# Linear attention with a routed MoE behind it: the division by the denominator for three of four query items moved from VectorE to ScalarE

## The chip, the cores and the metric

The kernel runs on one core of a Trainium2 chip. The metric is device time in microseconds (us) of one execution. The core's engines work in parallel, each through its own stream of instructions in the order of the program: TensorE (PE in the profile, PEld for its weight loads), VectorE (DVE), ScalarE (ACT), GpSimd (POOL) and SyncE (SP, which issues most DMAs). They wait for one another through semaphores.

## The reference

```python
# 8 batches, 8 heads, 576 rows, head dimension 64, 128 features
def phi(x):
    proj = einsum('bhsd,df->bhsf', x, w_phi)
    proj = proj - max(abs(proj), axis=-1, keepdims=True)
    return concatenate([exp(proj), exp(-proj)], axis=-1)
q_p, k_p = phi(q), phi(k)
kv  = einsum('bhsf,bhsd->bhfd', k_p, v)
z   = sum(k_p, axis=2)
num = einsum('bhsf,bhfd->bhsd', q_p, kv)
den = einsum('bhsf,bhf->bhs', q_p, z)[..., None] + 1e-06
attn = num / den
# x = attn as 4608 rows of 512; top-1 MoE of 8 experts, 512 -> 1024 -> 512:
do_compute = x @ w_skip > 0;  e = argmax(x @ w_gate);  g = softmax(x @ w_gate)[e]
out = x + (g * relu(x @ w1[e]) @ w2[e]  where do_compute, else 0)
```

The change concerns `num / den`.

## The kernel before, in words

The first 340 us or so are the attention, the rest is the MoE over sorted rows. A *unit* is four heads of one batch; there are 16 units of keys and 16 of queries. Each is cut into five *items*: item 0 holds the last 64 of the 576 rows of the heads, items 1 to 4 the other 512 (two head pairs, two halves of the rows). A loop over steps `t` works on one key item and, six steps later, on the query item of the same number: transposed by VectorE (tile `xT`), projected by TensorE (`ps_P`, L321), row maximum and subtraction by VectorE (`m` L328, `u` L331), exponentials by ScalarE (`ek` L346 and L347 for keys; `eqt` and `eq` L373 and L374 for queries, these after a transposition by TensorE into the PSUM tile `ps_U`, L367), products with `v` or `kva` by TensorE. `kva` is kv with 10 more columns: 9 for router and skip scores, and z. So five steps make a cycle of some 20 us, in which one unit of keys and one of queries go through.

A query item is used in `st_use_q` (L487; item 0 in L466, which runs for odd batches alone): TensorE fills one PSUM bank `ps_O` with four blocks of 74 columns (64 of num, 9 scores, 1 den). Then `norm` runs on it: VectorE adds 1e-6 to the four denominators (`den`, L438), takes the reciprocal (`rec`, L442), multiplies the 4 x 64 columns into `xm` (L449; `xt` for item 0) and the 4 x 9 score columns into `lgm` (L450). There are two banks `ps_O` in this stage. They turn between the items, the column sums of the keys (`z`, L407, copied out as `zs` by ScalarE, L410), the making of `kva` (L420, L424), and the ranking of rows for the MoE (L584). `ps_U` has one bank.

The order of TensorE's work in steps 8 to 78 is that of the program (`manual_schedule`); in it, L407 of a unit stands directly ahead of L487 of item 4. Everything else in the attention stage, so DVE, ACT, POOL and SP throughout and PE after step 78, is put in order by the framework's scheduler, which also adds the semaphore waits: an instruction that reads a PSUM bank is kept apart from an instruction of another engine on the same bank.

Behind the second unit of each batch, `post` computes the router's decisions (VectorE, nine small instructions and two for the gate), and, four steps later, `rank` (L584 on TensorE, then small VectorE instructions). Odd batches hold five row tiles there, even ones four. The MoE's weights come by SP in chunks of 512 KB; each is split into a rounded part by ScalarE (L198) and a rest by VectorE or GpSimd (L203). The first rows of the MoE are transposed in L782 and copied by ScalarE (L785) and VectorE (L786) before the first expert matmul (L908).

Of the kernel before, what the change touches and what calls it, by code (L numbers as in the profile page):

```python
# [12 lines left out]
AF = mybir.ActivationFunctionType  # L13
ALU = mybir.AluOpType
# [4 lines left out]
P = 128  # L19
# [5 lines left out]
def kernel(  # L25
# [12 lines left out]
    nc = tc.nc  # L38
    B, H, S, D = q.shape
# [40 lines left out]
    def bank(tag):  # L80
        if not ps:
            return psa.tile([P, 512], F32, tag=tag, name="ps_" + tag, bufs=CFG["na"][tag])
        return ps[0].tile([P, 512], F32, tag=tag, name="ps_" + tag, bufs=NB[tag])
# [146 lines left out]
    with actx:  # L230
# [200 lines left out]
                )  # L431
            kva_of[u.g] = kva

        def norm(o, xdst, ldst, shape):

            den = small.tile([P, 4], F32, tag="den", name="den")
            rec = small.tile([P, 4], F32, tag="rec", name="rec")
            nc.vector.tensor_scalar(  # L438
                out=den.rearrange("p (t o) -> p t o", o=1), in0=o[:, :, NA1:NAUG],
                scalar1=1e-6, scalar2=None, op0=ALU.add,  # L440
            )
            nc.vector.reciprocal(out=rec, in_=den)  # L442
            rv = rec.rearrange("p (t o) -> p t o", o=1)
            a, c = shape

            def sh(x):
                return x.rearrange("p (a c) d -> p a c d", a=a)

            nc.vector.tensor_tensor(out=xdst, in0=sh(o[:, :, 0:D]), in1=sh(rv.broadcast_to([P, 4, D])), op=ALU.mult)  # L449
            nc.vector.tensor_tensor(  # L450
                out=ldst, in0=sh(o[:, :, D:NA1]), in1=sh(rv.broadcast_to([P, 4, NA1 - D])), op=ALU.mult)

        def st_use_q(u, i):
            if i == 0 and u.b % 2 == 0:
                return
            kva = kva_of[u.g]
            o = bank("O")[:, 0:4 * NAUG]
            ov = o.rearrange("p (t c) -> p t c", c=NAUG)
            if i == 0:

                for h in range(4):
                    pr, hd = h // 2, h % 2
                    for half in range(2):
                        for par in range(2):
                            g = u.g - NQ * (1 - par)
                            nc.tensor.matmul(  # L466
                                ov[par * 64:par * 64 + 64, h, :],
                                et_of[g][:, half, hd * P + pr * 64:hd * P + pr * 64 + 64], kva_of[g][:, half, h, :],
                                start=(half == 0), stop=(half == 1),
                            )  # L470
                if u.hq == 0:
                    xt_of[u.b // 2] = (
                        [xp.tile([P, 1, 4 * D + 2 * h], F32, tag="xt%d" % h, name="xt") for h in range(2)],
                        xp.tile([P, 1, H, E + 1], F32, tag="lgt", name="lgt"),
                    )
                xt, lgt = xt_of[u.b // 2]
                norm(ov, xt[u.hq][:, 0, 0:4 * D].rearrange("p (h a d) -> p a h d", h=2, d=D),
                     lgt[:, 0, u.hq * 4:(u.hq + 1) * 4, :].rearrange("p (a h) e -> p a h e", a=2), (2, 2))
                return
            pr, th = (i - 1) // 2, (i - 1) % 2  # L480
            e = u.e[i].rearrange("p a (j h c) -> p a j h c", j=2, h=2)
            h0 = u.hq * 4 + 2 * pr
            for j in range(2):
                for hd in range(2):
                    for half in range(2):
                        for s in range(2):
                            nc.tensor.matmul(  # L487
                                ov[s * 64:s * 64 + 64, 2 * j + hd, :],
                                e[:, half, j, hd, s * 64:s * 64 + 64], kva[:, half, 2 * pr + hd, :],
                                start=(half == 0), stop=(half == 1),  # L490
                            )
            if u.hq == 0 and i == 1:
                xm_of[u.b] = (
                    [xp.tile([P, 4, 4 * D + 2 * h], F32, tag="xm%d" % h, name="xm") for h in range(2)],
                    xp.tile([P, 4, H, E + 1], F32, tag="lgm", name="lgm"),
                )
            xm, lgm = xm_of[u.b]
            norm(ov, xm[u.hq][:, 2 * th:2 * th + 2, 0:4 * D].rearrange(
                "p a (h r d) -> p a r h d", h=2, d=D)[:, :, pr],
                 lgm[:, 2 * th:2 * th + 2, h0:h0 + 2, :], (2, 2))  # L500
            if i == 4:
                c = slice(0, 4 * D)
                if u.hq == 0:
                    def store_half(b=u.b, xm=xm):
                        nc.sync.dma_start(out=rowm[b][:, :, c], in_=xm[0])
                        if b % 2 == 1:
                            nc.sync.dma_start(out=rowt[b // 2][:, c], in_=xt_of[b // 2][0][0][:, 0])
                    later.append((now[0] + 2, store_half))
                else:
                    post(u.b)  # L510
# [194 lines left out]
        for dh in range(2):  # L705
            nc.scalar.dma_start(
                out=wsrc[dh * 64:dh * 64 + 64],
                in_=w_phi)
# [9 lines left out]
        def f_use(u, i):  # L718
            (st_use_k if u.kind == "k" else st_use_q)(u, i)
# [382 lines left out]
    for grp in CFG["seq"]:  # L1102
# [7 lines left out]
        for which, w, n in how:  # L1110
            for _ in range(n):
                x = slots[which]
                c = done.get((x, w), 0)
# [82 lines left out]
    with tc.manual_schedule():  # L1196
# [4 lines left out]
        for k, (w, x, c) in enumerate(steps):  # L1201
            kind, i = x
# [95 lines left out]
```

## Time and profile before

| | |
|---|---|
| median of 3 runs | 623.17 us (622.9 to 623.51) |
| the profiled execution | 620.68 us, of which 619.0 us are its span |
| mean granted TensorE clock | 0.982 |
| busy in the span | PE 570.2 us, DVE 512.0, POOL 360.5, ACT 330.4 |

The profile shows one execution. Its views are the page (busy time of each engine, and the span in 40 slices), groups of instructions, the list of waits, windows (busy time per engine in a stretch), and a timeline. In timelines a row is: start, duration, engine, line and operation, tile written and tiles read, shapes, number of instructions merged, and in brackets the idle time of the engine before it with the instruction that ended it. TensorE's instructions overlap, so a row's end can lie behind the start of the next row.

### The profile page before, as it was taken

Reading aid. Unit: us, or ns where it says so; the run is one execution under the profiler, and the core shown is the slowest. Engines: PE = TensorE matmul, PEld = TensorE weight load, DVE = VectorE, ACT = ScalarE, POOL = GpSimd, SP = SyncE. Lnnn points to the kernel's source line nnn. Section 1 sums busy time; section 2 is a strip of 40 time slices with the busy share of each in tenths; the row PEclk is TensorE's granted clock in tenths of the full one; section 3 lists DMA queues with packets and bytes.
Section 4 is the critical chain, followed back from the end, with each engine's and each line's share of the span. In section 5 each row is a group of like instructions: output and inputs, shape, how many; then the busy total and the mean of one; then the engine's idle time right before and its main releaser. Section 6 shows DMA issues by size and latency. Waiting matters only on the chain. (4 is left out here: it accounts for less than half of the span.)

```text
span 619.0 us, 18767 instructions
## 1 busy us (share of the span) xinstructions
PE 570.2 (92%) x7486; PEld 468.9 (76%) x7486; DVE 512.0 (83%) x1084; ACT 330.4 (53%) x649; POOL 360.5 (58%) x390
## 2 busy tenths in 40 slices
PE   4699999999999999999999898699999898999993
PEld 2477777777777677776777788598888787989892
DVE  5899999999989999999986699957688887956851
ACT  3466556456656556556446445324658554665630
POOL 5665565564744747456661657974468855559121
PEclk9999999999999999999999898979999899999998
DMA  9988888887667766423152789676767678597200
GB/s 157 161 140 162 185 184 177 192 188 139 144 151 158 162 131 143 123 70 102 37 191 94 209 302 309 221 249 182 223 225 248 233 248 290 182 314 237 88 19 29
DMA packets 250233, 108.33 MB, mean 175 GB/s; under 512 B 192417, under 2 KB 235553, under 8 KB 250144
## 3 DMA queue, kind: packets, MB, share of 16 engines
q1 hardware_dynamic: 245632, 97.58, 60.9%
q0 software_dynamic: 3200, 9.45, 4.4%
q8 instruction: 60, 0.98, 0.6%
q10 hardware_dynamic: 1312, 0.08, 0.1%
q14 instruction: 29, 0.24, 0.1%
HBM read 83.86 MB, written 24.02 MB: 174 GB/s over the span
## 5 line engine op out<-in xcount | busy, mean ns | idle before, releaser
L203 POOL TENSOR_TENSOR w<-wraw_c,w 128x256 fp32r<-128x256 f32 x124 | 114.6, 958 | 51.1 <-ACT w L198 51.1
L354 POOL TENSOR_TENSOR z<-ek 128x512 f32<-128x512 f32 x64 | 81.5, 1273 | 98.4 <-ACT ek L347 73.6
L198 ACT ACTIVATE w<-wraw_c 128x1024 fp32r<-128x1024 f32 x96 | 97.5, 1051 | 4.3 <-DMA wraw_c<-in_moe_w_dram 2.9
L203 DVE TENSOR_TENSOR w<-wraw_c,w 128x1024 fp32r<-128x1024 f32 x65 | 86.9, 1345 | 12.9 <-ACT w L198 10.7
L328 DVE TENSOR_REDUCE m<-ps_P 128x8 f32<-128x1024 f32 (+2 forms) x86 | 88.6, 1030 | 6.4 <-PE ps_P L321 6.2
L331 DVE TENSOR_TENSOR u<-ps_P,m 128x1024 f32<-128x1024 f32 (+2 forms) x86 | 88.8, 1033 | 3.1 <-DVE xTt L296 0.2
L321 PE MATMUL ps_P<-wsrc,xT 64*64 64x128 f32 x2048 | 77.9, 281 | 12.1 <-DVE xT L298 6.9
L487 PEld LDWEIGHTS ps_O<-kva,eq 128*64 128x64 f32 x2048 | 74.5, 136 | 16.5 <-issue 5.7
L487 PE MATMUL ps_O<-kva,eq 128*64 128x74 f32 x2048 | 77.6, 228 | 4.1 <-DVE lgm L450 4.0
L321 PEld LDWEIGHTS ps_P<-wsrc,xT 64*64 64x64 f32 x2048 | 56.7, 134 | 27.4 <-issue 18.4
L373 ACT ACTIVATE eq<-ps_U 128x512 f32<-128x512 f32 x64 | 37.9, 592 | 64.7 <-PE ps_U L367 64.2
L389 PE MATMUL ps_K<-ek,v 128*64 128x256 f32 x512 | 70.8, 394 | 0.0
L855 POOL DMA_INDIRECT out_dram<-o,si x22 | 28.8, 1310 | 63.9 <-DVE si L854 56.8
L922 PE MATMUL ps_O<-w,hh 128*128 128x512 f32 x160 | 64.2, 401 | 0.0
L346 ACT ACTIVATE ek<-u 128x512 f32<-128x512 f32 x64 | 40.4, 631 | 38.4 <-DVE u L331 23.0
L367 PE MATMUL ps_U<-ident,u 128*128 128x128 f32 x288 | 49.1, 287 | 2.5 <-DVE u L331 1.9
L298 DVE STREAM_TRANSPOSE xT<-raw 128x512 f32<-128x512 f32 x64 | 44.8, 702 | 5.8 <-PE ps_P L321 2.8
L926 PE MATMUL ps_O<-w,hh 128*128 128x512 f32 x120 | 47.3, 394 | 1.3 <-POOL w L203 1.3
L389 PEld LDWEIGHTS ps_K<-ek,v 128*64 128x64 f32 x512 | 31.9, 137 | 20.9 <-issue 11.3
L927 PE MATMUL ps_O<-w,hlo 128*128 128x512 f32 x120 | 47.2, 393 | 0.0
L909 PE MATMUL ps_P<-x,w 128*128 128x256 f32 x144 | 38.9, 299 | 4.7 <-DVE x L786 4.7
L358 POOL TENSOR_TENSOR z<-z 128x512 f32<-128x512 f32 x32 | 40.8, 1275 | 2.5
(259 smaller groups left out, 1206.6 us busy)
## 6 DMA issues: line engine op xcount, KB each, us to landing
wraw_c<-in_moe_w_dram SPq DMA_DIRECT2D x96, 512.0 KB, 4.0
raw<-in_k_dram SPq DMA_DIRECT2D x64, 144.0 KB, 3.3
raw<-in_q_dram SPq DMA_DIRECT2D x64, 144.0 KB, 4.4
v<-in_v_dram SPq DMA_DIRECT2D x64, 128.0 KB, 2.8
out_dram<-xm SPq DMA_DIRECT2D x16, 512.0 KB, 4.2
xrows<-xm SPq DMA_DIRECT2D x8, 516.0 KB, 4.3
xrows<-xm SPq DMA_DIRECT2D x8, 512.0 KB, 4.7
vt<-in_v_dram SPq DMA_DIRECT2D x32, 32.0 KB, 2.8
```

The lines of the kernel that those rows point to most:

```text
L198: nc.scalar.activation(out=hi, in_=raw, func=AF.Copy)
L203: eng.tensor_tensor(out=lo[:, r], in0=raw[:, r], in1=hi[:, r].bitcast(F32), op=ALU.subtract)
L321: nc.tensor.matmul(p[s * 64:s * 64 + 64, hd, (nj + j) * NF:(nj + j + 1) * NF], xT[r, g * P + s * 64:g * P + s * 64 + 64], wsrc[r], start=T ...
L328: nc.vector.tensor_reduce(out=m.rearrange("p (j h) -> p j h", h=2), in_=pv, axis=AX.X, op=ALU.max, apply_absolute_value=True)
L331: nc.vector.tensor_tensor(out=uu[:, 0:2 * nj, :].rearrange("p (j h) f -> p j h f", h=2), in0=pv, in1=m.rearrange("p (j h o) -> p j h o", h ...
L354: zeng.tensor_tensor(out=z, in0=e[:, 0:2, :], in1=e[:, 2:4, :], op=ALU.add)
L367: nc.tensor.transpose(t[:, tt * P:(tt + 1) * P], uu[:, tt, :], ident)
L389: nc.tensor.matmul(o[hd * 64:hd * 64 + 64, :], u.v[:, 2 * hd + pr, g * D:(g + 1) * D], u.e[i][:, 2 * j + hd, :], start=(g == 0), stop=False,)
L487: nc.tensor.matmul(ov[s * 64:s * 64 + 64, 2 * j + hd, :], e[:, half, j, hd, s * 64:s * 64 + 64], kva[:, half, 2 * pr + hd, :], start=(half ...
L922: nc.tensor.matmul(y[sub], hh[:, t], wh[:, fi, :], start=first, stop=False)
L926: nc.tensor.matmul(y[sub], hh[:, t], wl[:, fi, :], start=False, stop=False)
L927: nc.tensor.matmul(y[sub], hlo[:, t], wh[:, fi, :], start=False, stop=last)
```

## The change

For query items 1, 2 and 3 (not 0 and 4) the product L449 is replaced by four ScalarE instructions, one a head, each copying 64 columns from PSUM to `xm` with the reciprocal as scale. `den`, `rec` and `lgm` stay on VectorE. Line numbers behind it move by five (L450 becomes L455, L487 becomes L492, L563 becomes L568).

```diff
-        def norm(o, xdst, ldst, shape):
+        def norm(o, xdst, ldst, shape, act=False):
...
-            nc.vector.tensor_tensor(out=xdst, in0=sh(o[:, :, 0:D]), in1=sh(rv.broadcast_to([P, 4, D])), op=ALU.mult)
+            if act:
+                for j in range(4):
+                    nc.scalar.activation(out=xdst[:, j // c, j % c], in_=o[:, j, 0:D], func=AF.Copy, scale=rec[:, j:j + 1])
+            else:
+                nc.vector.tensor_tensor(
+                    out=xdst, in0=sh(o[:, :, 0:D]), in1=sh(rv.broadcast_to([P, 4, D])), op=ALU.mult)
             nc.vector.tensor_tensor(
                 out=ldst, in0=sh(o[:, :, D:NA1]), in1=sh(rv.broadcast_to([P, 4, NA1 - D])), op=ALU.mult)
...
-                 lgm[:, 2 * th:2 * th + 2, h0:h0 + 2, :], (2, 2))
+                 lgm[:, 2 * th:2 * th + 2, h0:h0 + 2, :], (2, 2), i in (1, 2, 3))
```

The scheduler then puts the instructions in another order. First VectorE, from the norm of item 2 to the norm of item 3 in one cycle. `[waits ...]` names the engines whose semaphores an instruction waits for; DVE_49 is VectorE's own, Activation_49 that of ScalarE. Before:

```order
L438 TENSOR_SCALAR den<-ps_O 128x4 [waits PE_49]
L442 RECIPROCAL rec<-den 128x4 [waits DVE_49]
L449 TENSOR_TENSOR xm<-ps_O,rec 128x2x2x64 [waits DVE_49]
L450 TENSOR_TENSOR lgm<-ps_O,rec 128x2x18
L298 STREAM_TRANSPOSE xT<-raw 128x512 [waits PE_49]
L328 TENSOR_REDUCE m<-ps_P 128x8 [waits PE_49]
L331 TENSOR_TENSOR u<-ps_P,m 128x1024 [waits DVE_49,Activation_49]
L438 TENSOR_SCALAR den<-ps_O 128x4 [waits PE_49]
L442 RECIPROCAL rec<-den 128x4 [waits DVE_49]
L449 TENSOR_TENSOR xm<-ps_O,rec 128x2x2x64 [waits DVE_49]
L450 TENSOR_TENSOR lgm<-ps_O,rec 128x2x18
L328 TENSOR_REDUCE m<-ps_P 128x8 [waits PE_49]
```

The same stretch of VectorE after:

```order
L438 TENSOR_SCALAR den<-ps_O 128x4 [waits PE_49]
L442 RECIPROCAL rec<-den 128x4 [waits DVE_49]
L298 STREAM_TRANSPOSE xT<-raw 128x512 [waits PE_49]
L455 TENSOR_TENSOR lgm<-ps_O,rec 128x2x18 [waits DVE_49,Activation_49]
L328 TENSOR_REDUCE m<-ps_P 128x8 [waits PE_49]
L331 TENSOR_TENSOR u<-ps_P,m 128x1024 [waits DVE_49]
L438 TENSOR_SCALAR den<-ps_O 128x4 [waits PE_49]
L442 RECIPROCAL rec<-den 128x4 [waits DVE_49]
L455 TENSOR_TENSOR lgm<-ps_O,rec 128x2x18 [waits DVE_49,Activation_49]
L328 TENSOR_REDUCE m<-ps_P 128x8 [waits PE_49]
```

The two products are gone, `lgm` of the changed items waits for ScalarE, and the transposition `xT` has moved ahead of `lgm` of item 2.

Second ScalarE, from the exponentials of a key item to the copy of `zs`, which is where item 3 falls. Before:

```order
L346 ACTIVATE ek<-u 128x4x128 [waits DVE_49]
L347 ACTIVATE ek<-u 128x4x128
L373 ACTIVATE eqt<-ps_U 128x256 [waits PE_49]
L374 ACTIVATE eqt<-ps_U 128x256
L410 ACTIVATE zs<-ps_O 128x256 [waits PE_49]
```

The same stretch of ScalarE after, which stands so in all cycles but the last:

```order
L346 ACTIVATE ek<-u 128x4x128 [waits DVE_49,Activation_49]
L347 ACTIVATE ek<-u 128x4x128
L373 ACTIVATE eqt<-ps_U 128x256 [waits PE_49]
L374 ACTIVATE eqt<-ps_U 128x256
L451 ACTIVATE xm<-ps_O,rec 128x64 [waits DVE_49]
L451 ACTIVATE xm<-ps_O,rec 128x64 x3
L410 ACTIVATE zs<-ps_O 128x256 [waits PE_49]
```

The four copies of item 3 stand behind `ek` and `eqt`; those of items 1 and 2 stand, in nearly all cycles, between or beside the two exponentials `eq` (L373 and L374) of a later query item.

Third ScalarE at the end of the attention, where the last query unit meets the first weights of the MoE. Before:

```order
L374 ACTIVATE eq<-ps_U 128x512
L198 ACTIVATE w<-wraw_c 128x1024 x4
L785 ACTIVATE x<-ps_U 128x4x128 x2
L547 ACTIVATE ex<-d 128x40
L785 ACTIVATE x<-ps_U 128x4x128 x2
```

The same place of ScalarE after:

```order
L374 ACTIVATE eq<-ps_U 128x512
L198 ACTIVATE w<-wraw_c 128x1024 x4
L451 ACTIVATE xm<-ps_O,rec 128x64 x8
L552 ACTIVATE ex<-d 128x40
L790 ACTIVATE x<-ps_U 128x4x128 x4
```

The copies of items 2 and 3 of the last unit stand behind four splits of weights, and all four `x` of the first expert rows behind `ex` of the last batch's router. On VectorE one split (L203) stands there ahead of the two `lgm`. On SP the store of the last batch's rows moves behind two loads of weights and four stores of `out`.

## The prediction

> **What bounds the kernel now.** I read the page first, then windows of 25 us, then the waits of the attention stage (25 to 340 us), then the timeline of one quiet cycle. The page's first row and two windows (columns: PE, PEld, DVE, ACT, POOL busy, granted clock, DMA share, GB/s):
>
> ```profile
> PE 570.2 (92%) x7486; PEld 468.9 (76%) x7486; DVE 512.0 (83%) x1084; ACT 330.4 (53%) x649; POOL 360.5 (58%) x390
> 50.00:75.00 25.00, 25.00 (x464) 19.33 (x464) 23.10 (x53) 14.38 (x35) 12.46 (x10) 1.00 0.87 167
> 275.00:300.00 25.00, 22.86 (x441) 17.57 (x439) 24.22 (x69) 14.15 (x33) 15.15 (x16) 1.00 0.21 70
> ```
>
> In the quiet window TensorE never pauses and VectorE is idle 1.9 us of 25. In the window with routing work VectorE is busiest (24.22) and TensorE idles 2.1 us. ScalarE has over 10 us free in both. So a shorter VectorE can give back only TensorE's idle time. The waits name it (waiting instruction, releaser, total us, times, longest):
>
> ```profile
> PE ps_O L487 <- DVE lgm L450: 4.0, 3, 1.4
> PE ps_O L584 <- DVE lgm L450: 2.2, 3, 0.7
> ACT ek L346 <- DVE u L331: 18.1, 15, 2.9
> ```
>
> TensorE waited 6.2 us for VectorE to release `ps_O`, in three cycles only (the ones after odd batches). That is about all the change can win. ScalarE, on its side, takes up `ek` as soon as VectorE has made `u`.
>
> **The change part by part.** What is removed, and the instruction that stays behind it:
>
> ```profile
> L449 DVE TENSOR_TENSOR xm<-ps_O,rec 128x256 f32<-128x256 f32 x64 | 27.1, 424 | 2.1 <-DVE rec L442 0.3
> L450 DVE TENSOR_TENSOR lgm<-ps_O,rec 128x36 f32<-128x36 f32 x64 | 11.8, 185 | 0.0
> ```
>
> 48 of 64 products go: 48 x 0.424 = 20.4 us of VectorE's busy time. Added are 192 ScalarE copies of 64 columns, four in a group. No row shows a copy with a column of reciprocals as scale. The nearest are the copies of `kva` from PSUM:
>
> ```profile
> 68.24 0.41 ACT L425 ACTIVATE kva<-ps_O 128x292 f32<-128x292 f32 x1
> 68.53 0.19 ACT L428 ACTIVATE kva<-ps_O 128x4 f32<-128x4 f32 x1
> 68.69 0.41 ACT L425 ACTIVATE kva<-ps_O 128x292 f32<-128x292 f32 x1
> ```
>
> 292 columns take 0.41 us and 4 take 0.19, so 64 take 0.24; the next starts 0.16 after the 4-column one, so 0.21 after one of 64. A group of four is then 3 x 0.21 + 0.24 = 0.87 us. If they overlap as the exponentials do (below: 0.60 long, next after 0.47, so 0.13 hidden) it is 0.6; with no overlap 4 x 0.24 = 0.96. I take 0.87, from the smallest copies. 48 groups are 42 us of ScalarE, which its idle time can hold. [...]
>
> What matters is not the load but the wait. In the new order `lgm` waits for ScalarE, and in VectorE's queue everything stands behind it: the next `m` and `u`, on which `ek` waits. [...] So the product is off VectorE's busy time but not off its path: where `lgm` came 0.34 us after `xm` began, it now comes after a group of 0.87 on an engine that may have other work. The quiet cycle before, TensorE first, then VectorE, then ScalarE:
>
> ```profile
> 58.82 1.10 PE L321 MATMUL ps_P<-wsrc,xT 64*64 64x128 f32 x32
> 61.20 1.20 PE L487 MATMUL ps_O<-kva,eq 128*64 128x74 f32 x32
> 63.73 0.64 PE L407 MATMUL ps_O<-z,ones_f 128*32 128x256 f32 x8
> 64.30 1.25 PE L487 MATMUL ps_O<-kva,eq 128*64 128x74 f32 x32
> ```
> ```profile
> 55.10 0.18 DVE L442 RECIPROCAL rec<-den 128x4 f32<-128x4 f32 x1
> ...
> 56.33 0.96 DVE L328 TENSOR_REDUCE m<-ps_P 128x6 f32<-128x768 f32 x1 [0.49 <-PE ps_P L321]
> ...
> 57.43 0.92 DVE L331 TENSOR_TENSOR u<-ps_P,m 128x768 f32<-128x768 f32 x1
> ...
> 58.55 0.18 DVE L442 RECIPROCAL rec<-den 128x4 f32<-128x4 f32 x1
> ...
> 59.55 0.71 DVE L298 STREAM_TRANSPOSE xT<-raw 128x512 f32<-128x512 f32 x1 [0.27 <-PE ps_P L321]
> 60.19 1.19 DVE L328 TENSOR_REDUCE m<-ps_P 128x8 f32<-128x1024 f32 x1
> 61.48 1.23 DVE L331 TENSOR_TENSOR u<-ps_P,m 128x1024 f32<-128x1024 f32 x1
> ...
> 62.81 0.18 DVE L442 RECIPROCAL rec<-den 128x4 f32<-128x4 f32 x1
> ...
> 63.36 0.18 DVE L450 TENSOR_TENSOR lgm<-ps_O,rec 128x36 f32<-128x36 f32 x1
> ```
> ```profile
> 55.58 0.58 ACT L373 ACTIVATE eq<-ps_U 128x512 f32<-128x512 f32 x1
> 56.05 0.59 ACT L374 ACTIVATE eq<-ps_U 128x512 f32<-128x512 f32 x1
> ...
> 58.99 0.60 ACT L373 ACTIVATE eq<-ps_U 128x512 f32<-128x512 f32 x1 [2.25 <-PE ps_U L367]
> ...
> 62.74 0.63 ACT L346 ACTIVATE ek<-u 128x512 f32<-128x512 f32 x1 [0.73 <-DVE u L331]
> ...
> 63.80 0.36 ACT L373 ACTIVATE eqt<-ps_U 128x256 f32<-128x256 f32 x1
> 64.06 0.37 ACT L374 ACTIVATE eqt<-ps_U 128x256 f32<-128x256 f32 x1
> ```
>
> The same cycle after, hop by hop (0.1 from ScalarE to VectorE and for the small steps between; 0.05 from `rec` to ScalarE):
> - Item 1: `rec` is there at 55.28, ScalarE free behind its first `eq` at 56.05. Group to 56.92, `lgm` at 57.0, `m` at 57.1 instead of 56.33. `u` follows 1.1 later (57.43 - 56.33): 58.2 to 59.1. `rec` of item 2 ends 0.38 behind `u`, as before (58.73 behind 58.35): 59.5.
> - Item 2: group 59.55 to 60.42, `lgm` 60.5, `m` 60.6 instead of 60.19. `xT` fits into this wait, so it costs nothing here. `u` 1.29 after `m`: 61.9 to 63.1.
> - Item 3: `ek` at 63.15, `eqt` ends 1.69 later as before (62.74 to 64.43), the group starts 0.1 ahead of that end: 64.74 to 65.61; `lgm` 65.7 to 65.88. TensorE's L487 of item 4 needs that bank (the one of item 3, since L407 has the other). Release 0.15 behind: 66.03 instead of 64.30.
>
> TensorE stalls 1.75 us in a quiet cycle, with nothing in its queue to fill it, and as it was never idle there the cycle grows by that. ScalarE's idle time covers the other uses: the `eq` exponentials that are delayed by a group had 2.25 us of idle time ahead of L373. With a group of 0.6 the stall is 1.2, with 0.96 it is 2.05.
>
> 13 cycles in TensorE's written order meet L487 of items 3 and 4:
> - 7 quiet ones: 7 x 1.75 = 12.3 us.
> - 3 with the ranking of an even batch: `xT` stands behind `lgm` of item 2 there, so its 0.64 (59.55 to 60.19) is no longer hidden, and some 0.35 of small ranking steps are added: 2.75 each, 8.3 us.
> - 3 with an odd batch, late before already: the wait at item 4 grows by 1.75, that at L584 by 0.63 (0.87 + 0.1 in place of the product's 0.34), both on top of the 0.7 and 1.4 seen: 2.4 each, 7.2 us.
>
> The last two cycles and the last query unit, where PE's order is the scheduler's: an estimate of 3 us, from two stalls of 1.5 (0 to 4). Then the end of the attention:
>
> ```profile
> 335.37 3.63 PE L487 MATMUL ps_O<-kva,eq 128*64 128x74 f32 x96
> 344.70 0.56 PE L909 MATMUL ps_P<-x,w 128*128 128x256 f32 x1
> 336.50 3.90 ACT L198 ACTIVATE w<-wraw_c 128x1024 fp32r<-128x1024 f32 x4
> 340.49 1.72 DVE L203 TENSOR_TENSOR w<-wraw_c,w 128x1024 fp32r<-128x1024 f32 x1 [0.52 <-POOL w L203]
> ```
>
> The three L487 of the first row follow each other at 1.2 us. Now the third needs item 2's bank, whose copies stand behind the four splits (340.4) and whose `lgm` behind the split on VectorE (342.2): it starts at 342.5, not 337.8, 4.7 late. The router's `ex`, the `x` copies and the experts, steady from 344.70, come after it. I take 4.5; 0 if the first weights are late anyway, 6 with the later `x`. The two loads of weights that SP now issues ahead of the last store only gain; behind these, the MoE is as before.
>
> Sum: 12.3 + 8.3 + 7.2 + 3 + 4.5 = 35.3 us. Against the profiled execution's own 620.68: 656.0; against the median of the runs, 2.5 higher, 623.17 + 35.3 = 658.5.
>
> **The rivals.**
> - *Faster: the group hides.* TensorE's 6.2 us of waits go, the time is 617. It speaks for this that ScalarE is half idle and VectorE saturated where those waits are. It decides at `lgm` of item 3: the group would have to end by 63.3, and `eqt` ahead of it in the queue ends at 64.43. Chance 0.05.
> - *Only item 3 costs.* If VectorE gains enough lead from TensorE's stalls to hide items 1 and 2, the chain is `eqt` 64.43 - 0.1 + 0.87 + 0.43 (`lgm` and its hops) = 65.6: 1.3 a cycle, 17 us, less the 6.2, plus 3 for the end: 637. Against it: `m` in quiet cycles already waits for TensorE, so a lead is of no use there. Chance 0.14.
> - *The clock drops as well.* After long waits TensorE ran slow:
>
> ```profile
> 393.30 0.50 PE L926 MATMUL ps_O<-w,hh 128*128 128x512 f32 x1 [1.28 <-POOL w L203]
> 395.00:400.00 5.00, 3.46 (x19) 2.69 (x17) 4.97 (x4) 2.98 (x4) 5.00 (x4) 1.00 0.87 292
> 403.17 0.58 PE L909 MATMUL ps_P<-x,w 128*128 128x256 f32 x1 [4.71 <-DVE x L786]
> 405.00:410.00 5.00, 5.00 (x61) 4.91 (x60) 1.41 (x3) 1.52 (x2) 4.51 (x8) 0.58 0.76 229
> ```
>
> A wait of 1.28 us left the clock at 1.00, one of 4.71 brought it to 0.58 for 5 us, a loss of 2.1. My six long stalls (2.7 to 3.2) lie between: 6 x 2.1 = 12.6, so 671. [...] Chance 0.10.
> - *No effect*, if ScalarE's groups and `lgm` land where `xm` and `lgm` did: 623. `rec` to `lgm` is 0.55 now (62.81 to 63.36), less than a group. Chance 0.03.
>
> **How the numbers follow.** The forecast, VectorE held behind ScalarE in every cycle, has 0.68, and 658.5 is its sum. Its own range: groups of 0.6, with nothing for the end, 13 x 0.55 = 7 less and 7.5 less, 644; groups of 0.96, 13 x 0.3 = 4 more and 2.5 more for the end, 665. To leave out no more than 2 in 10 the range reaches down to the second rival and up to just short of the third: 636 to 669. A measurement of this kernel tells about 0.2% (1.2 us) from no change. Slower: 0.68 + 0.14 + 0.10 = 0.92; same 0.03; faster 0.05.
>
> **What would show it.** Right: `lgm` L455 on VectorE idle before it, waiting for ScalarE's `xm`; TensorE's waits for `lgm` in L492 up from 4.0 us to over 20, in all cycles, about 1.75 each; VectorE's busy time down by 20 us and ScalarE's up by some 40; a copy of 0.24 us every 0.21; the first L913/L914 run 35 us later than 344.70; the MoE behind it as long as before. Wrong: `lgm` not idle, or the waits at L492 only in the routing cycles, or a stage clock below 1.00, or copies over 0.3 us apart.

## The result, and the profile after

The changed kernel takes 668.86 us (median of 4 runs, 665.28 to 673.09), against 623.34 for the kernel before beside it: a ratio of 1.075, 95% interval 1.070 to 1.080. The forecast was 658.5. The direction and the waits came out as forecast, but the time is 10 us above the sum. The range ended at 669: 668.86 lies just below that, and the ratio on the 623.17 that the range started from (670) just above it. Nearest is the third rival, in which TensorE's clock drops as well (671). The profiled execution took 670.12 us, 668.4 of them its span, 49.4 more than the span before.

The page's first row and its row of granted clocks, then the two windows that the prediction showed of before (columns as there):

```profile
PE 585.1 (88%) x7486; PEld 479.1 (72%) x7486; DVE 496.5 (74%) x1036; ACT 367.9 (55%) x841; POOL 356.7 (53%) x390
...
PEclk9899979979989999899899979997999999999998
50.00:75.00 25.00, 23.32 (x414) 17.72 (x405) 19.95 (x39) 16.20 (x46) 11.45 (x9) 1.00 0.90 176
275.00:300.00 25.00, 21.45 (x388) 17.04 (x388) 17.02 (x36) 15.92 (x47) 11.22 (x10) 0.93 0.43 102
```

VectorE lost 15.5 us of busy time (512.0 to 496.5) and ScalarE got 37.5 more, but in the quiet window TensorE, which never paused before, now idles 1.7 us. In the other window it idles 3.6, and the clock there is 0.93, where it was 1.00: one of the signs that the prediction had named as showing it wrong. TensorE is even *busier* in all (570.2 to 585.1) with the same 7486 matmuls: some of them ran slowly (the 32 of L492 at 91.15 in 2.24 us, those at 67.98 in 1.25).

The groups of the change, from the page, and the waits from 25 to 382 us:

```profile
L451 ACT ACTIVATE xm<-ps_O,rec 128x64 f32<-128x64 f32 x192 | 44.3, 322 | 18.5 <-DVE rec L442 14.2
...
L455 DVE TENSOR_TENSOR lgm<-ps_O,rec 128x36 f32<-128x36 f32 x64 | 12.2, 192 | 54.9 <-ACT xm L451 54.9
```
```profile
DVE lgm L455 <- ACT xm L451: 54.9, 37, 2.4
PE ps_O L492 <- DVE lgm L455: 30.2, 13, 3.1
...
PE ps_O L589 <- DVE lgm L455: 4.4, 3, 1.5
```

VectorE's small score product, which never waited before, stands 54.9 us idle for ScalarE. TensorE's wait for that product was 6.2 us (4.0 + 2.2) and is 34.6. The same quiet cycle as in the prediction, the second half of it, ScalarE, VectorE and TensorE:

```profile
65.10 0.63 ACT L346 ACTIVATE ek<-u 128x512 f32<-128x512 f32 x1 [0.70 <-DVE den L438]
65.63 0.62 ACT L347 ACTIVATE ek<-u 128x512 f32<-128x512 f32 x1
66.15 0.36 ACT L373 ACTIVATE eqt<-ps_U 128x256 f32<-128x256 f32 x1
66.42 0.37 ACT L374 ACTIVATE eqt<-ps_U 128x256 f32<-128x256 f32 x1
66.68 0.93 ACT L451 ACTIVATE xm<-ps_O,rec 128x64 f32<-128x64 f32 x4
```
```profile
65.11 0.18 DVE L442 RECIPROCAL rec<-den 128x4 f32<-128x4 f32 x1
67.64 0.20 DVE L455 TENSOR_TENSOR lgm<-ps_O,rec 128x36 f32<-128x36 f32 x1 [2.36 <-ACT xm L451]
```
```profile
65.72 0.64 PE L407 MATMUL ps_O<-z,ones_f 128*32 128x256 f32 x8
67.98 1.21 PE L492 MATMUL ps_O<-kva,eq 128*64 128x74 f32 x31 [1.63 <-DVE lgm L455]
```

`rec` of item 3 is there at 65.29. ScalarE begins the copies at 66.68, since `ek` and `eqt` stand ahead of them in its queue. VectorE waits through all of it, with the next `m` behind the wait in its queue, and TensorE finds the bank closed for 1.63 us.

### The profile page after: what moved, and what is told of

It reads as the page before. It is cut to its first block, busy times and chain, and to the rows that moved or that the text cites. A ratio compares the mean times of both kernels' runs of the same rounds, so it can differ in the third digit from the quotient of the medians.

```text
span 668.4 us, 18918 instructions
## 1 busy us (share of the span) xinstructions
PE 585.1 (88%) x7486; PEld 479.1 (72%) x7486; DVE 496.5 (74%) x1036; ACT 367.9 (55%) x841; POOL 356.7 (53%) x390
## 5 line engine op out<-in xcount | busy, mean ns | idle before, releaser
L203 POOL TENSOR_TENSOR w<-wraw_c,w 128x256 fp32r<-128x256 f32 x124 | 111.0, 930 | 52.1 <-ACT w L198 52.0
L492 PE MATMUL ps_O<-kva,eq 128*64 128x74 f32 x2048 | 82.6, 235 | 36.4 <-DVE lgm L455 34.9
L492 PEld LDWEIGHTS ps_O<-kva,eq 128*64 128x64 f32 x2048 | 78.7, 143 | 49.7 <-issue 41.7
L203 DVE TENSOR_TENSOR w<-wraw_c,w 128x1024 fp32r<-128x1024 f32 x65 | 86.2, 1335 | 14.6 <-ACT w L198 11.7
L321 PE MATMUL ps_P<-wsrc,xT 64*64 64x128 f32 x2048 | 83.2, 293 | 10.5 <-DVE xT L298 7.0
L321 PEld LDWEIGHTS ps_P<-wsrc,xT 64*64 64x64 f32 x2048 | 60.6, 142 | 27.0 <-issue 19.0
L373 ACT ACTIVATE eq<-ps_U 128x512 f32<-128x512 f32 x64 | 38.0, 594 | 66.1 <-PE ps_U L367 65.9
L389 PE MATMUL ps_K<-ek,v 128*64 128x256 f32 x512 | 72.6, 400 | 0.0
L451 ACT ACTIVATE xm<-ps_O,rec 128x64 f32<-128x64 f32 x192 | 44.3, 322 | 18.5 <-DVE rec L442 14.2
L367 PE MATMUL ps_U<-ident,u 128*128 128x128 f32 x288 | 51.7, 300 | 1.7 <-ACT eqt L374 1.3
L455 DVE TENSOR_TENSOR lgm<-ps_O,rec 128x36 f32<-128x36 f32 x64 | 12.2, 192 | 54.9 <-ACT xm L451 54.9
## 6 DMA issues: line engine op xcount, KB each, us to landing
wraw_c<-in_moe_w_dram SPq DMA_DIRECT2D x96, 512.0 KB, 4.7
out_dram<-xm SPq DMA_DIRECT2D x16, 512.0 KB, 4.7
xrows<-xm SPq DMA_DIRECT2D x8, 512.0 KB, 4.8
```

Source lines behind the costliest of these rows:

```text
L203: eng.tensor_tensor(out=lo[:, r], in0=raw[:, r], in1=hi[:, r].bitcast(F32), op=ALU.subtract)
L321: nc.tensor.matmul(p[s * 64:s * 64 + 64, hd, (nj + j) * NF:(nj + j + 1) * NF], xT[r, g * P + s * 64:g * P + s * 64 + 64], wsrc[r], start=T ...
L367: nc.tensor.transpose(t[:, tt * P:(tt + 1) * P], uu[:, tt, :], ident)
L389: nc.tensor.matmul(o[hd * 64:hd * 64 + 64, :], u.v[:, 2 * hd + pr, g * D:(g + 1) * D], u.e[i][:, 2 * j + hd, :], start=(g == 0), stop=False,)
L492: nc.tensor.matmul(ov[s * 64:s * 64 + 64, 2 * j + hd, :], e[:, half, j, hd, s * 64:s * 64 + 64], kva[:, half, 2 * pr + hd, :], start=(half ...
```

## The experiments

Each shows its edit against the changed kernel, what was expected, and what came out. The ratios are to the kernel before on the same chip, whose median was 622.79, 621.11 or 622.11 us; each heading or its first lines say which.

### Item 3 alone (beside 622.79)

```diff
-                 lgm[:, 2 * th:2 * th + 2, h0:h0 + 2, :], (2, 2), i in (1, 2, 3))
+                 lgm[:, 2 * th:2 * th + 2, h0:h0 + 2, :], (2, 2), i == 3)
```

> ScalarE's copies only for item 3 of every four; items 1 and 2 go back to VectorE. Theory A (VectorE's lgm product must wait until ScalarE has left the same bank, and ScalarE works in order: at item 3 its group stands behind the copies of ek and eqt, so VectorE, and TensorE behind it, are held): item 3 of a quiet cycle still costs about 1.4 us, a ranking cycle about 2 to 2.4, and the end of attention about 4; TensorE's waits for lgm at item 3 stay near 1.6 and 2 to 3 us; the time is 640 to 650. Rival B (each of the three items costs the same share of the 45.5 us): 638 at most, with waits for lgm at item 3 of about 0.6 us.

Measured: 649.15 us, ratio 1.044 (1.039 to 1.050). Its waits from 25 to 365 us:

```profile
PE ps_O L492 <- DVE lgm L455: 24.0, 13, 3.3
PE ps_O L589 <- DVE lgm L455: 2.2, 3, 0.7
```

A quiet cycle's wait is 1.26 us, those of the ranking cycles are 1.7 to 3.3. Item 3 alone makes more than half of the loss, inside theory A's range. The wait at L589 is as before: that one belongs to item 1.

### Items 1 and 2 alone (beside 622.79)

```diff
-                 lgm[:, 2 * th:2 * th + 2, h0:h0 + 2, :], (2, 2), i in (1, 2, 3))
+                 lgm[:, 2 * th:2 * th + 2, h0:h0 + 2, :], (2, 2), i in (1, 2))
```

> ScalarE's copies only for items 1 and 2 of every four; item 3 goes back to VectorE. Theory A: no wait of TensorE for lgm in the quiet cycles, about 0.7 to 1.5 us in the ranking cycles, the end of attention still 4 us later; granted clock back at about 1.00 there; the time is 627 to 634. Rival B (what counts is ScalarE's added load or the number of copies): two thirds of the 45.5 us stay, about 653.

Measured: 632.47 us, ratio 1.016 (1.010 to 1.022), as theory A had it. It keeps two thirds of the added copies and a fifth of the loss, so the loss does not go by the number of copies or by ScalarE's load. TensorE has no wait for `lgm` in a quiet cycle; those in ranking cycles are 1.0 to 1.8, and the steady stream of expert matmuls (the first L914 of an unbroken row, L909 before) begins 24.2 us behind the last L407, against 19.3 before.

### Item 1 alone (beside 621.11), item 2 alone (beside 622.11)

Two kernels, with one of the two added lines each:

```diff
-                 lgm[:, 2 * th:2 * th + 2, h0:h0 + 2, :], (2, 2), i in (1, 2, 3))
+                 lgm[:, 2 * th:2 * th + 2, h0:h0 + 2, :], (2, 2), i == 1)
+                 lgm[:, 2 * th:2 * th + 2, h0:h0 + 2, :], (2, 2), i == 2)
```

> ScalarE's copies for item 1 of every four only, in the changed order (copies ahead of lgm). Theory: nothing stands ahead of item 1's copies in ScalarE's queue in the quiet cycles, and 0 to 1 us in the ranking cycles; up to 3 us there and 0 to 4 at the end: 623 to 629. Rival (each item a third of the loss): 638.

> ScalarE's copies for item 2 of every four only, in the changed order (copies ahead of lgm). Theory: in ScalarE's queue two eq copies stand ahead of item 2's, no ek, so VectorE's wait is short and falls in slack; the cost is at the end of attention (items 1 and 2 cost 4.8 us there, item 1 alone 1.2): 624 to 628. Rival (additive thirds): 638.

Measured: item 1 630.07 us, ratio 1.015 (1.013 to 1.017), above what I expected; item 2 622.36, ratio 1.001 (0.9995 to 1.003), just under it. The miss on item 1 is in its queue. VectorE's timeline in a ranking cycle, then ScalarE's:

```profile
77.22 0.18 DVE L442 RECIPROCAL rec<-den 128x4 f32<-128x4 f32 x1
79.27 0.20 DVE L455 TENSOR_TENSOR lgm<-ps_O,rec 128x36 f32<-128x36 f32 x1 [1.88 <-ACT xm L451]
```
```profile
77.21 0.42 ACT L346 ACTIVATE ekt<-u 128x256 f32<-128x256 f32 x1 [1.96 <-DVE den L438]
77.53 0.40 ACT L347 ACTIVATE ekt<-u 128x256 f32<-128x256 f32 x1
77.84 0.58 ACT L373 ACTIVATE eq<-ps_U 128x512 f32<-128x512 f32 x1
78.32 0.92 ACT L451 ACTIVATE xm<-ps_O,rec 128x64 f32<-128x64 f32 x4
```

Two `ekt` and an `eq` stand ahead of item 1's copies, where I had expected nothing in quiet cycles and up to 1 us in ranking ones. VectorE waits 1.88 us here, and 1.73 in a quiet cycle. In quiet cycles it makes that up: TensorE waits for no `lgm` there. In ranking cycles it has nothing to make it up with (24.2 of 25 us busy before), and is still late 8 us on, where TensorE waits for the product of item 3, which VectorE makes alone here:

```profile
87.04 1.25 PE L492 MATMUL ps_O<-kva,eq 128*64 128x74 f32 x32 [1.12 <-DVE lgm L455]
```

So the three items alone cost 27.6, 9.3 and 0.7 us by their ratios (of 622.79, 621.11 and 622.11), 37.6 together, where the change as a whole costs 45.5. The 8 that are over appear only when the delays come together, and the traces say that most of it is TensorE's clock: between 25 us and the last L407 it falls six times in the changed kernel (twice for 6.83 us and four times for 3.41, some 10 us of cost, two sections below), twice with item 3 alone (3.41 us each, some 2.6 of cost) and never with item 1 or item 2 alone.

### The score product ahead of the copies (beside 622.79)

`scores` is the product that makes `lgm`, as a function of its own:

```diff
             if act:
+                scores()
                 for j in range(4):
...
-            nc.vector.tensor_tensor(
-                out=ldst, in0=sh(o[:, :, D:NA1]), in1=sh(rv.broadcast_to([P, 4, NA1 - D])), op=ALU.mult)
+            if not act:
+                scores()
```

> All three items as in the changed kernel, but VectorE's lgm product is written ahead of ScalarE's four copies, so that ScalarE waits for VectorE and not the other way round. Theory A1 (the whole loss is VectorE's wait in front of lgm): TensorE's waits for lgm are gone and the time is 623 or less. Theory A2 (also the bank that item 3 holds comes free late, since its copies still stand behind ek and eqt in ScalarE's queue, and the next transposes need the bank): TensorE waits about 1.1 us in each quiet cycle on xm in place of lgm; 640 to 645. Rival B (ScalarE's load itself): 665 to 670.

Measured: 638.65 us, ratio 1.027 (1.019 to 1.034): theory A2, a little under its range. All 192 copies are there. Those of item 3 have the same place in ScalarE's queue; the scheduler puts those of item 1 one `eq` later, and those of item 2 behind the `eq` and two `ek`. So at items 1 and 2 more than the wait changed, at item 3 the wait alone. 30 us of the loss are gone. What is left at TensorE is the bank, now held by the copies (25 to 365 us), and the quiet cycle of above, 0.94 us for 1.63:

```profile
PE ps_O L497 <- ACT xm L456: 20.0, 14, 4.7
```
```profile
66.86 1.25 PE L497 MATMUL ps_O<-kva,eq 128*64 128x74 f32 x32 [0.94 <-ACT xm L456]
```

The longest, 4.7, is in the last unit, behind the splits of the first expert weights. The other 15.3 stand against 34.6 in the changed kernel, 19.3 less. None is over 1.84 us, and the clock stays at 1.00 in all these cycles, which is worth the 10 us of the next section: together nearly all of the 30.

### The same z matmuls three times over, to fill the wait (beside 622.79)

```diff
-            for h in range(4):
+            for h in 3 * list(range(4)):
                 nc.tensor.matmul(zb[h * 32:(h + 1) * 32, 0:2 * NF], ones_f, u.z[2 + 2 * (h // 2)][:, h % 2, :],
```

> The changed kernel, with the four z matmuls of line 407 issued three times over (the same values written again), so that TensorE has about 1.1 us of work inside the stretch in which it else waits for lgm. If about 10 us of the loss are the clock that falls to 0.50 after waits of 3 us: the waits at line 492 shrink to about 0.5 and 1.9 us, the clock stays near 1.00 behind them, and the time falls to 657 to 662 in spite of the added work. If the clock has no part in it: 668 or above.

Measured: 661.89 us, ratio 1.064 (1.059 to 1.070). With 256 matmuls more the kernel is faster than the changed one. The waits got shorter (L492 30.2 to 17.9, and L589 4.4 to 2.6; 0.77 in a quiet cycle and 1.89 to 2.27 in a ranking one, a little more than expected), but the added work takes that back: from L407 to L407, the two kinds of cycle in which neither kernel has a low clock take 21.79 and 22.36 us in the changed kernel, and 22.77 and 21.78 here. What is gained lies in the cycles with a low clock. Three cycles hold the ranking of an even batch. The time from TensorE's L492 behind the wait to its next L407, the same work each time and with no wait between, was 19.42, 19.52 and 19.51 us before; in the changed kernel it is 21.98, 20.81 and 20.81; here it is 19.53, 20.83 and 19.53; and with item 3 alone 19.53 three times. The first of the changed kernel:

```profile
91.15 2.24 PE L492 MATMUL ps_O<-kva,eq 128*64 128x74 f32 x32 [3.02 <-DVE lgm L455]
...
113.13 0.64 PE L407 MATMUL ps_O<-z,ones_f 128*32 128x256 f32 x8
```

32 matmuls took 2.24 us where 1.25 is usual. Now TensorE's windows, cut at the points where the clock changes (columns: length, PE busy, matmuls, granted clock, DMA share, GB/s). The changed kernel first:

```profile
45.89:49.30 3.41, 1.90 (x40) 1.00 0.97 203
49.30:52.71 3.41, 3.38 (x50) 1.00 0.87 142
...
86.86:90.27 3.41, 1.27 (x36) 1.00 0.67 189
90.27:93.68 3.41, 2.53 (x34) 0.50 0.56 125
93.68:97.10 3.42, 3.42 (x39) 0.50 1.10 178
...
182.43:185.84 3.41, 0.33 (x13) 1.00 0.12 26
185.84:189.25 3.41, 3.41 (x48) 0.50 0.35 59
```

Item 3 alone, then the filled kernel:

```profile
129.57:132.98 3.41, 1.55 (x40) 1.00 0.54 122
132.98:136.40 3.42, 2.02 (x44) 1.00 0.02 5
...
218.31:221.72 3.41, 0.35 (x11) 1.00 0.08 18
221.72:225.14 3.42, 3.42 (x48) 0.50 0.37 61
```
```profile
181.46:184.87 3.41, 1.46 (x38) 1.00 0.02 6
184.87:188.28 3.41, 3.41 (x40) 0.51 0.72 114
```

In these traces the clock changes only on a grid of 3.41 us (every low spell that lies between 25 and 376 us in the twelve traces lasts 3.41 or 6.83), and a stretch is at 1.00 or at 0.50 (0.51 where my window is not exact). In these rows what follows a stretch goes by how much TensorE worked in it: 1.27, 0.33, 0.35 and 1.46 us of 3.41 are followed by 0.50, and 1.90, 1.55 and 2.02 are not. The wait of 3.26 us with item 3 alone was cut by the grid into two stretches with 1.86 and 1.40 of pause, and cost no clock; one of 3.34 us fell almost whole into one stretch (218.31), and did. A stretch with 43% of work (1.46 of 3.41) was still followed by 0.50. In the changed kernel all six waits of 3.0 to 3.1 us were followed by a low stretch: twice of 6.83 us, which cost 2.4 each (21.98 - 19.53 is the one shown), and four times of 3.41, which cost about 1.3 each (20.81 - 19.53).

### The last unit as before (beside 621.11)

```diff
-                 lgm[:, 2 * th:2 * th + 2, h0:h0 + 2, :], (2, 2), i in (1, 2, 3))
+                 lgm[:, 2 * th:2 * th + 2, h0:h0 + 2, :], (2, 2), i in (1, 2, 3) and u.g < NU - 1)
```

> The changed kernel, but the last of the 16 query units as before (no copies by ScalarE there). Theory: the wait of 4.7 us at the last matmuls of attention and the low clock behind it go, 4.5 to 7 us less than the changed kernel: 662 to 664.5. Rival: the last unit costs nothing, since the work behind it is limited elsewhere: 668 to 670.

Measured: 662.03 us, ratio 1.066 (1.064 to 1.069); by the ratios 5.4 us less than the changed kernel's 1.075. The end of attention in the changed kernel, TensorE and ScalarE, and then TensorE here:

```profile
385.12 2.24 PE L492 MATMUL ps_O<-kva,eq 128*64 128x74 f32 x32 [4.69 <-DVE lgm L455]
...
393.00 0.56 PE L914 MATMUL ps_P<-x,w 128*128 128x256 f32 x1
```
```profile
379.15 3.93 ACT L198 ACTIVATE w<-wraw_c 128x1024 fp32r<-128x1024 f32 x4
382.94 1.78 ACT L451 ACTIVATE xm<-ps_O,rec 128x64 f32<-128x64 f32 x8
```
```profile
379.14 3.63 PE L492 MATMUL ps_O<-kva,eq 128*64 128x74 f32 x96
...
388.83 0.56 PE L914 MATMUL ps_P<-x,w 128*128 128x256 f32 x1
```

From the last L407 to the steady L914 it is 25.0 us in the changed kernel (368.01 to 393.00), 18.9 here (369.92 to 388.83), and 19.3 before.

### Looking for a faster kernel: the product first, without item 3

Items 1 and 2 (beside 621.11), the same without the last unit (beside 621.11), and item 2 alone without the last unit (beside 622.11). All have `scores()` ahead of the copies, and one of the three added lines each, in this order:

```diff
-                 lgm[:, 2 * th:2 * th + 2, h0:h0 + 2, :], (2, 2), i in (1, 2, 3))
+                 lgm[:, 2 * th:2 * th + 2, h0:h0 + 2, :], (2, 2), i in (1, 2))
+                 lgm[:, 2 * th:2 * th + 2, h0:h0 + 2, :], (2, 2), i in (1, 2) and u.g < NU - 1)
+                 lgm[:, 2 * th:2 * th + 2, h0:h0 + 2, :], (2, 2), i == 2 and u.g < NU - 1)
```

> ScalarE's copies for items 1 and 2 only, and VectorE's lgm product written ahead of them, so that VectorE never waits for a copy. Theory: all waits of TensorE for lgm up to the last unit go (the kernel with items 1 and 2 in the changed order lost 6.7 us up to the last unit), but the last unit still has its copies behind ScalarE's w copies, or VectorE's x later, and costs about 4 to 5; 622 to 629. Rival (the copies' release of the PSUM banks comes too late at items 1 and 2 as well): 632 or above, with waits for xm at line 497.

> As the kernel with lgm first and items 1 and 2, but the last of the 16 query units as in the kernel before. Theory: the end of attention is as before, so 3 to 5 us less than its neighbour, 618 to 624; it beats the kernel before only if VectorE's relief (32 x 4 products fewer) takes the 0.7 and 1.4 us waits for lgm in the ranking cycles away, up to 6 us. Rival: equal to its neighbour (the end of attention does not matter).

> lgm first, and ScalarE's copies for item 2 only, not in the last unit. Item 1 keeps VectorE's product, so the wait of 1.73 us for its copies at line 594 (items 1 and 2 done so) should shrink to the 0.7 us of the kernel before; item 2's product (0.34 us) leaves VectorE, so the 1.3 us wait at line 487 of the odd batches should shrink by 0.34 or more. Theory: 1 to 3 us below the kernel before at the most (618 to 621 against 621). Rival (the copies' later release of item 2's bank costs as much as VectorE gains): equal to the kernel before.

Measured: 622.96 us, ratio 1.0036 (1.0014 to 1.0058); 621.95, ratio 1.0025 (1.0006 to 1.0044); 619.90, ratio 0.9969 (0.9954 to 0.9983). The last unit is worth at most 1 us here, less than the 3 to 5 expected, and the intervals of the two overlap, so the rival holds there. In the first, TensorE's waits of 6.2 us for `lgm` became waits for the copies of item 1, whose bank L594 needs; in the third, they are back at 0.7 there, and the other one shrank from 4.0 to 3.2 (25 to 345 us, first kernel, then third):

```profile
PE ps_O L594 <- ACT xm L456: 5.7, 6, 1.7
```
```profile
PE ps_O L497 <- DVE lgm L450: 3.2, 3, 1.1
PE ps_O L594 <- DVE lgm L450: 2.2, 3, 0.7
```

The third is 0.3% faster than the kernel before, 1.9 us, with an interval of 0.2 to 0.5%.

## Why the prediction was wrong, and what of it was right

The step that failed is the clock. The sum of 35.3 us has no term for it: the six long stalls stand in it at their length alone. All six were followed by a low clock, which cost some 10 us.

**Right: the mechanism of the waits.** VectorE's `lgm` waits behind a group of copies that waits in ScalarE's queue. In the quiet cycle VectorE waits 1.72, 0.17 and 2.36 us at items 1, 2 and 3, where the hop by hop comes to some 1.7, 0.3 (beside `xT`) and 2.2. Writing the short product first took away about two thirds of the loss (45.5 to 15.9). What is left of it is item 3's bank, which opens late behind `ek` and `eqt` (0.94 us in a quiet cycle), and the last unit.

**Right: the sizes of the waits.** In the 13 cycles I had 27.8 us. Measured are 34.6 - 6.2 = 28.4: six quiet cycles with 1.63 and one with 1.93 (I had 1.75), three even batches with 3.02 to 3.08 (2.75), three odd ones with 3.02 to 3.13 and 1.46 (3.1 and 1.3 with what was there before). The sum is closer than its parts: quiet cycles came out shorter and even batches longer than I had them, which is luck. The group of copies, which no row of before showed, took 0.92 us (I had 0.87). One copy is 0.32 long, not 0.24, and the next begins (0.92 - 0.32) / 3 = 0.20 later, so the group came out near my value by a wrong split. VectorE's busy time fell by 15.5 and ScalarE's rose by 37.5, where I had 20 and some 40.

**Undersized, but by little: the end of attention**, 5.7 (25.0 - 19.3) for 4.5. The stretch behind the wait of 4.69 ran at a low clock as well (L492 took 2.24). The rest of the MoE grew by 1.1, where I had 0.

**Wrong: the clock.** I counted all six waits of 2.7 to 3.2 us at their length alone, and gave the rival in which the clock drops too a chance of 0.10, with 12.6 us. It dropped behind all six. Of the two rows that I showed, a wait of 1.28 without a drop and one of 4.71 with it, neither says on which side 3.0 lies. Other rows of the same trace do. In the kernel before, a single wait of 1.60 us in the MoE left 1.70 of work in its stretch, and the next stretch was at 0.50:

```profile
484.34:487.75 3.41, 1.70 (x7) 1.00 0.92 314
487.75:491.16 3.41, 3.10 (x7) 0.50 0.51 172
486.67 0.50 PE L846 MATMUL ps_O<-w,hh 128*128 128x512 f32 x1 [1.60 <-POOL w L203]
```

Two more waits of 1.41 and 1.63 us share the stretch from 340.98, 1.30 of work, and the next one is at 0.50 too. A stall of 3 us that the grid cuts in two leaves at least 1.5 us of pause in one half, so these rows made a drop behind most of the six the likelier case. That the six would leave the clock at 1.00 no run had shown. The cost is some 10 us (2 x 2.4 + 4 x 1.3), nearly what that rival said. Of the 49.4 us by which the span grew, 28.4 are the waits, 10 the clock, and 5.7 and 1.1 what comes behind the last L407. The remaining 4.2 are no measured term but what is left: about 0.3 a cycle beside the waits (the 13 cycles, L407 to L407, grew by 42.4), and 0.4 in the last cycle; I had 3 for the last two cycles.

The clock also fits the spread: the four runs of the changed kernel range over 7.8 us, those of the kernel before beside them over 0.9 (over 4.4 in its 23 runs beside item 1 alone, 618.4 to 622.8), and the longer the run, the lower its mean clock (665.28 at 0.965, 673.09 at 0.951). That the place of the waits on the grid decides this from run to run is an inference. Two traces show it once: up to the last unit the kernel with the last unit as before runs the same instructions in the same order as the changed one, and its first long wait (1.92 us, 1.93 there) fell into one stretch, where in the changed kernel it was cut in two (45.89, above, no drop):

```profile
45.50:48.91 3.41, 1.49 (x40) 1.00 0.89 183
48.91:52.32 3.41, 3.41 (x51) 0.50 0.86 146
```

**The rivals.** "Only item 3 costs" had 1.3 us a cycle, 17 in all, less the 6.2. Its quiet cycle is right for item 3 alone (1.26 measured), but the waits there grew by 20.0 us (24.0 + 2.2 - 6.2), not 10.8, since the ranking cycles have up to 3.34; and items 1 and 2 add to it in all cycles (1.63 for 1.26 in a quiet one). "The group hides" (617) is what became of item 2 alone, without the last unit, once the product stood first: no wait of TensorE for its copies shows, and the kernel gained 1.9 us.

## What to carry to other kernels

Before work is moved to an idle engine, look at what stands ahead of it in that engine's queue at that moment, and at who then waits for it: ScalarE was idle for 45% of the span and was still the late one. Where two engines read the same bank, write the short read that others wait for first; here the kernel in that order kept only a third of the loss. A wait of the bounding engine can cost more than its length: here a stretch of 3.41 us with 1.50 us of matmuls or less was followed by a low clock. As an estimate from these runs, price a wait of 2 us or more with a low stretch on top (some 1.3 us here), and where a wait lies between two rows, one with a drop behind it and one without, look up every low stretch of the trace and what stood ahead of it.

## What the runs showed of the hardware that I had not expected

- TensorE's granted clock changed only on a fixed grid of 3.41 us. In the twelve traces from 25 to 380 us, and in those of before and of the changed kernel to the end, every stretch at 1.00 with 1.50 us of matmuls or less was followed by 0.50. Of those with 1.55 to 2.2 (1.86 to 1.2 of pause) most were followed by 1.00, but five by 0.50 (1.70 and 1.80 in the kernel before, 1.66 with items 1 and 2 alone, 2.07 with the last unit as before, 1.80 with the product first and item 2 alone), two of them before the last L407, so that edge is not sharp.
- The way back took more work: in the same stretches of trace, every stretch at 0.50 with 2.67 us of matmuls or less was followed by another low one, every one with 2.88 or more by 1.00.
- Whether a pause cost clock went by its place as well as its length: of three pauses of 1.89, 1.95 and 1.94 us in the filled kernel, only the one within a single stretch did. Behind two waits of 3.02 us in the changed kernel the low clock lasted two stretches, 6.83 us; in the first of the two cases the first low stretch had 2.53 us of matmuls and 0.88 of pause (90.27, above).
- Extra matmuls made a kernel faster: 256 more of them, written into the pauses, took 7 us off the changed kernel.
